# A linear-attention block and an MLP on one core: key weights folded once, first two pairs in 128-row products, a new order of the first stage

## The chip, the core and the metric

The kernel runs on one core of a Trainium2 chip. The metric is device time in microseconds (us), the median of the runs: 389.91 us before the change (3 runs, 389.55 to 390.11). Five engines work side by side, each through its own list of instructions in order: TensorE (PE; its weight loads are PEld), VectorE (DVE), ScalarE (ACT), GpSimd (POOL) and SyncE (SP), which only issues DMA transfers. ACT and POOL issue a few transfers too.

## The reference

x has 2048 rows (tokens) of 576 columns, 32 heads of 18 columns. All data are bfloat16.

```python
def _A_ref(x, wqkv, w_phi, wo):                       # H = 32, Dh = 18
    qkv = (x @ wqkv).reshape(B, S, 3, H, Dh).transpose(2, 0, 3, 1, 4)
    q, k, v = qkv[0], qkv[1], qkv[2]
    pq = einsum("bhsd,hdf->bhsf", q, w_phi)
    pk = einsum("bhsd,hdf->bhsf", k, w_phi)
    phi_q = concatenate([softmax(pq), softmax(-pq)], axis=-1)
    phi_k = concatenate([softmax(pk), softmax(-pk)], axis=-1)
    kv = einsum("bhsf,bhsd->bhfd", phi_k, v)          # over all tokens
    z  = einsum("bhsf->bhf", phi_k)
    num = einsum("bhqf,bhfd->bhqd", phi_q, kv)
    den = einsum("bhqf,bhf->bhq", phi_q, z)[..., None] + 1e-6
    return (num / den).transpose(0, 2, 1, 3).reshape(B, S, D) @ wo

def _B_ref(x, w1, b1, w2, b2):                        # 576 -> 4608 -> 576
    return gelu(layernorm(x) @ w1 + b1) @ w2 + b2

h  = x + _A_ref(layernorm(x), A_wqkv, A_w_phi, A_wo)
h2 = h + _B_ref(layernorm(h), B_w1, B_b1, B_w2, B_b2)
```

kv and z sum over all tokens, so no token's output can be finished before every token's keys and values are done.

## The kernel before

The 2048 tokens are 16 tiles of 128, handled as 8 pairs p = 0 to 7. The program has a first stage (mixer up to the state kv), a short tail that finishes the first pair, and the MLP blocks, between which the other pairs' mixer outputs are finished.

**Weights.** w_phi is folded into the key and query weights, so that x yields pk and pq in one product. For that the weights must lie transposed. The key weights wk are loaded and turned on PE (`flip_mm`, L377, evicted by `flip_ev`, L383), the query weights come through transposing DMAs (`turn_wq`, L159). `spread` (L231) makes the block-diagonal bd out of w_phi. `fold_k_mm` (L405) multiplies the turned key weights with bd for nine blocks of 128 rows of the folded weight wkp: blocks 0 to 3 are rows 0 to 511, blocks 4 to 7 the rows from 64 on, block 8 the last and the first 64. Both layouts are made by products. For the queries `fold_mm` (L419) makes five blocks, and `swap_q` (L434 to L438) copies the halves crosswise by DMA.

**A pair.** Layer norm: `stats` (DVE, L312 and L313), `power` (POOL), `centre` (POOL), `scale` (DVE L335 or ACT L290). Its result lies with the two token tiles interleaved in chunks of 64 columns, and is turned by a DMA (`turn_dma`, L342) or, for pair 0, by nine PE transposes (`turn_x_mm`, L359). Then the products, each 18 matmuls of 64 rows by 128 columns against 288 columns of weights (`project`, L450): a row half of the array works for each token tile, so two such matmuls run side by side. One such group is called a product here: `value_mm`, `key_mm`, `query_mm`, two per pair (the two halves of the heads). ACT evicts: `value_ev` (L460), `key_exp` and `query_exp` (two exponentials per product, L472). `key_sum` on DVE is a reduction (L501) and a reciprocal (L503), `key_weigh` divides (POOL or DVE, L507). `sums(p, a)` adds one token tile to the state in PSUM with 11 matmuls (L586).

**Tail.** After the last `sums`, `table` (DVE) copies the state; `combine_mm` (L673) and `divide` (DVE, L686) make the mixer output of pair 0, `turn_o_mm` turns it, `residual_mm` (L722) multiplies by wo, `residual_add`, `residual_stats`, `second`, `rescale` and `turn2_mm` prepare the MLP's input; `up` begins (L1161). Eight query products are left over to fill PE during this chain.

**Order.** Each engine's list follows an order written out by hand in the program (some 350 lines of calls), for all five engines. PSUM for the first stage is a pool `two` of three buffers of two banks each, handed out in turn; keys' exponentials have five buffers. `filler(n)` are n matmuls of no use that keep PE busy while it would wait. The space of the transposed and folded weights is that of the first half of w1, so `load_w1(0, ...)` can start only after the folds. The second half of w1 and w2 take the space of the values and keys, so they start after the last `sums` (`close_keys`).

Of the kernel before, what the change touches and what calls it, by code (L numbers as in the profile page):

```python
# [8 lines left out]
P = 128  # L9
# [6 lines left out]
D = 576  # L16
# [4 lines left out]
NC = 5  # L21
# [19 lines left out]
B1R = (NM + 15) // 16 * 16  # L41
GAP = P - COUNT[-1] * 2 * DH
# [3 lines left out]
def kernel(  # L46
# [43 lines left out]
    def leave_home(key):  # L90
# [22 lines left out]
        tc.tile_pool(name="two", bufs=3, space=bass.MemoryType.PSUM, reuse_waits="tile")  # L113
# [4 lines left out]
    exk_pool = kctx.enter_context(tc.tile_pool(name="exk_pool", bufs=5, side="left"))  # L118
# [15 lines left out]
    wTk = borrowed(NG, D).rearrange("p (g f) -> p g f", g=NG)  # L134
# [29 lines left out]
    def load_wk(part, eng):  # L164
        if part:
            eng.dma_start(wk[0:KH, 4, :], A_wqkv[512:D, D : 2 * D])
# [8 lines left out]
    def load_values(part, eng):  # L175
        if part < 2:
            eng.dma_start(
                wv[:, 4 * part : 4 * part + 4, :],
                A_wqkv[part * KH : part * KH + 512, 2 * D : 3 * D].rearrange(
# [4 lines left out]
        r0 = 512 if part == 2 else 0  # L184
        eng.dma_start(
            wv[(part - 2) * KH : (part - 1) * KH, 8, :], A_wqkv[r0 : r0 + KH, 2 * D : 3 * D]
        )
# [6 lines left out]
    def load_phi(eng):  # L194
        two_rows = wphi_rows[0 : 2 * 252, :].rearrange("(g p) f -> p g f", p=252)
        eng.dma_start(wph[:, 0:4:2, :], two_rows[0:P, :, :])
        eng.dma_start(wph[:, 1:4:2, :], two_rows[252 - P : 252, :, :])
        eng.dma_start(wph[0:72, 4, :], wphi_rows[504:576, :])
# [3 lines left out]
    load_phi(nc.scalar)  # L202
# [53 lines left out]

    def filler(n):
# [6 lines left out]
    def warm(n):  # L264
        pw = two.tile([P, 4, P], FP32, name="pw", tag="two")
        wide = ident[:, :].rearrange("p (o f) -> p o f", o=1).to_broadcast([P, 4, P])
        for _ in range(n):
            nc.tensor.matmul(pw[:, :, :], ident[:, :], wide, start=True, stop=True)

# [59 lines left out]
    def scale(p, i, eng):  # L329
        mv, rs = moments[p][:2]  # L330
        dst, src = lnb[p % 3][:, :, i, :], chunks(2 * p + i)
        if eng is act:
# [16 lines left out]
    def transposes(key, src, home=None):  # L349
# [3 lines left out]
        else:  # L353
            parts = [
                two.tile([P, 5 - e, P], BF16, name="pT", tag="two")[:, :, :] for e in range(2)
# [7 lines left out]
    def turned_back(key, dst, part, copy):  # L363
        copy(dst[:, 5 * part : 5 + 4 * part, :], flight[key][part])  # L364

# [5 lines left out]

    def flip_mm(g):
        f0, m = g * 126 - 2 * (g % 2), P if g < NG - 1 else 72
        pX = flight["w", g] = two.tile([P, DP], BF16, name="pX", tag="two")
        for c in range(NC):
            k = P if c < NC - 1 else KH
            nc.tensor.transpose(  # L377
                pX[:m, c * P : c * P + k], wk[:k, c, f0 : f0 + m], ident[:k, :k]
            )

    def flip_ev(g, copy):
        m = P if g < NG - 1 else 72
        copy(wTk[:m, g, :], flight["w", g][:m, 0:D])  # L383
# [3 lines left out]
    def folded_part(g, name, c, rows):  # L387
        n = GH[g] * DH
        flat = flight[name, c].rearrange("p b f -> p (b f)")
        return flat[rows, SPAN + g * 126 : SPAN + g * 126 + n]  # L390

    def folded_whole(name, c, m):
        return flight[name, c].rearrange("p b f -> p (b f)")[:m, SPAN : SPAN + D]

    def fold_k_mm(n):
        flight["k", n] = two.tile([P, 2, 512], FP32, name="pW", tag="two")[:, :, :]
        if n < 8:
            f0 = n // 4 * KH + n % 4 * P
            parts = [(slice(0, P), slice(f0, f0 + P))]
        else:  # L400
            parts = [(slice(0, KH), slice(512, D)), (slice(KH, P), slice(0, KH))]
        for g in range(NG):
            k = P if g < NG - 1 else 72
            for rows, fs in parts:
                nc.tensor.matmul(  # L405
                    folded_part(g, "k", n, rows), wTk[:k, g, fs],
                    bd[:k, g, 0 : GH[g], :].rearrange("p h f -> p (h f)"),
                    start=True, stop=True,
                )

    def fold_k_ev(n, copy):
# [909 lines left out]
```

## Time and profile before

| | |
|---|---|
| runs before, median | 389.91 us (389.55 to 390.11) |
| profiled execution, span | 391.7 us |
| first product of a value (PE) | 15.69 us |
| end of the last `sums` | 66.96 us |
| start of the MLP's first matmul | 86.00 us |
| PE busy | 383.0 us |

The profiled execution's own time is its span; it is 1.8 us above the median of the runs. A row of a view in order of time has the start, the length, the engine and the line, and in square brackets the idle time ahead and what ended it. In rows of groups, `x16 | 21.0, 1312 | 1.7` is 16 instructions, 21.0 us busy, 1312 ns mean, 1.7 us idle ahead. q8 is the DMA queue that brings instructions.

### The profile page before, as it was taken

What the parts mean: (1) busy time and instruction counts of PE and PEld (TensorE: products, weight loads), DVE (VectorE), ACT (ScalarE), POOL (GpSimd) and SP (SyncE); (2) the same over time, 40 slices, a digit from 0 to 9 for tenths busy, and PEclk for the clock granted to TensorE, in tenths of its full rate; (3) what the DMA queues carried; (4) which work ended last, traced back from release to release, by engine and by line L of the source; (5) the groups of instructions that cost most, each with busy time, mean ns of one, the idle gap of its engine ahead of it and who ended that gap; (6) DMA issues with size and microseconds to landing.
All of it is one profiled execution on the core that took longest, in us unless ns stands there. A gap on an engine that the chain in (4) does not pass through costs nothing.

```text
span 391.7 us, 10190 instructions
## 1 busy us (share of the span) xinstructions
PE 383.0 (98%) x4475; PEld 269.0 (69%) x4475; DVE 166.0 (42%) x364; ACT 163.2 (42%) x291; POOL 117.8 (30%) x161
## 2 busy tenths in 40 slices
PE   7999999799999999999999999999999999999997
PEld 3778779479978887844457887444677764447773
DVE  6998997385249388590019322000480000000100
ACT  2998995478500850046650000666300016661000
POOL 6399998116404654144003111000031110000120
PEclk9999999899999999999999999999999999999999
DMA  8977599999455578433003462000071000000000
GB/s 250 259 128 128 93 218 188 238 313 248 148 105 102 98 105 136 94 66 68 2 2 62 89 108 48 17 1 2 2 105 47 17 15 2 2 2 0 17 28 19
DMA packets 74096, 34.93 MB, mean 89 GB/s; under 512 B 61028, under 2 KB 71524, under 8 KB 74052
## 3 DMA queue, kind: packets, MB, share of 16 engines
q1 hardware_dynamic: 72944, 32.78, 40.3%
q0 software_dynamic: 336, 1.33, 1.2%
q8 instruction: 35, 0.57, 0.7%
q10 hardware_dynamic: 772, 0.17, 0.2%
q14 instruction: 9, 0.07, 0.1%
HBM read 16.47 MB, written 2.36 MB: 48 GB/s over the span
## 4 chain that ended last, share of the span: by engine, by line
PE 93%; ACT 2%; DMA 2%; issue 1%; DVE 1%; SPq 0%
PE po L1205 36%; PE ph L1161 36%; PE pk L450 8%; PE pv L450 5%; PE pa L722 4%; DMA w<-in_A_wqkv_dram 2%; PE acc_kv L586 1%; PE pn L673 1%; ACT home L472 1%; ACT shared L412 0%; DVE xh L731 0%; PE pW L419 0%; PE pW L405 0%; PE pT L359 0%; PE pX L377 0%
## 5 line engine op out<-in xcount | busy, mean ns | idle before, releaser
L1183 ACT ACTIVATE home<-ph,b1col 128x512 bf16<-128x512 f32 (+1 forms) x180 | 98.4, 598 | 169.1 <-PE ph L1161 165.9
L1205 PE MATMUL po<-w,home 128*128 128x288 bf16 (+2 forms) x1152 | 143.3, 286 | 0.0
L1161 PE MATMUL ph<-shared,w 64*128 64x512 bf16 (+2 forms) x1638 | 141.3, 331 | 0.6 <-ACT shared L364 0.6
L1205 PEld LDWEIGHTS <-home 128*128 128x128 bf16 x1152 | 109.4, 98 | 32.1 <-issue 1.8
L1161 PEld LDWEIGHTS <-w 64*128 64x128 bf16 x1638 | 80.3, 94 | 60.5 <-issue 0.7
L1209 DVE TENSOR_TENSOR ot<-po,hb 128x288 bf16<-128x288 f32 (+2 forms) x32 | 14.4, 453 | 106.4 <-PE po L1205 96.7
L450 PEld LDWEIGHTS <-home 64*128 64x128 bf16 x864 | 42.9, 95 | 13.6 <-issue 3.3
L1194 POOL TENSOR_TENSOR hb<-xh,b2bc 128x576 f32<-128x576 bf16 x16 | 20.4, 1273 | 104.6 <-DVE ot L1209 102.8
L536 POOL TENSOR_TENSOR padded<-home,rq 128x540 bf16<-128x540 bf16 x32 | 34.9, 1102 | 34.5 <-DVE rq L528 18.9
L731 DVE TENSOR_TENSOR xh<-pa,xh 128x288 bf16<-128x288 f32 x32 | 13.0, 447 | 72.4 <-PE pa L722 72.4
L274 POOL TENSOR_TENSOR rs<-va,mhalf 128x1 f32<-128x1 f32 x16 | 8.8, 549 | 110.9 <-DVE va L272 110.9
L507 POOL TENSOR_TENSOR phik<-phik,rk 128x576 bf16<-128x576 bf16 x28 | 33.4, 1218 | 1.4 <-DVE rk L503 1.2
L472 ACT ACTIVATE home<-pk 128x576 bf16<-128x576 f32 x32 | 18.6, 665 | 12.7 <-PE pk L450 10.4
L450 PE MATMUL pk<-wqp,home 64*128 64x288 bf16 x288 | 20.5, 293 | 2.8 <-issue 2.8
L501 DVE TENSOR_REDUCE sk<-phik 128x64 f32<-128x1152 bf16 x16 | 21.0, 1312 | 1.7 <-ACT phik L472 1.6
L527 DVE TENSOR_REDUCE sk<-home 128x64 f32<-128x1152 bf16 x16 | 21.0, 1310 | 0.0
L686 DVE RECIPROCAL rec<-pn 128x18 f32<-128x18 f32 (+1 forms) x32 | 8.0, 249 | 28.5 <-PE pn L673 28.5
L450 PE MATMUL pv<-wv,home 64*128 64x288 bf16 x288 | 19.6, 283 | 0.0
L472 ACT ACTIVATE phik<-pk 128x576 bf16<-128x576 f32 x32 | 18.7, 656 | 1.8 <-PE pk L450 1.1
L450 PE MATMUL pk<-shared,home 64*128 64x288 bf16 x288 | 19.3, 283 | 0.0
L722 PE MATMUL pa<-wo,shared 64*128 64x288 bf16 x288 | 18.6, 283 | 0.0
L722 PEld LDWEIGHTS <-shared 64*128 64x128 bf16 x288 | 13.9, 94 | 4.5 <-issue 0.5
(76 smaller groups left out, 208.3 us busy)
## 6 DMA issues: line engine op xcount, KB each, us to landing
w<-in_B_w_dram SPq DMA_DIRECT2D x21, 432.0 KB, 8.7
out_dram<-ot SPq DMA_DIRECT2D x15, 144.0 KB, 2.2
xh<-in_A_x_dram SPq DMA_DIRECT2D x3, 576.0 KB, 6.8
wo<-in_A_wo_dram SPq DMA_DIRECT2D x4, 324.0 KB, 8.0
w<-in_B_w_dram POOLq DMA_DIRECT2D x3, 432.0 KB, 13.0
wv<-in_A_wqkv_dram SPq DMA_DIRECT2D x2, 576.0 KB, 8.7
w<-in_A_wqkv_dram SPq DMA_DIRECT2D x1, 576.0 KB, 6.0
wqp<-wqp SPq DMA_DIRECT2D x2, 288.0 KB, 3.9
```

The lines of the kernel that those rows point to most:

```text
L450: nc.tensor.matmul(dst[:, a, 0:HALF], lhs[rows, c, :], w[rows, slot, i * HALF : (i + 1) * HALF], start=(n == 0), stop=(n == KC - 1),)
L472: nc.scalar.activation(rows[:, :, i * HH : (i + 1) * HH, s, :], flight[key, p, i][:, :, 0:HALF].rearrange("p a (h f) -> p a h f", f=DH), A ...
L501: nc.vector.tensor_reduce(sk[:, :, :], part_of(dst, i), AX.X, ALU.add)
L507: eng.tensor_tensor(part, part, flight["r" + key, p, i][:, a, :].rearrange("p (h o) -> p h o", o=1).to_broadcast([P, NH, DH]), ALU.mult,)
L527: nc.vector.tensor_reduce(sk[:, :, :], part_of(phiq[p], i), AX.X, ALU.add)
L536: eng.tensor_tensor(padded[:, a, g0 * P : (g0 + 5) * P].rearrange("p (g k) -> p g k", k=P)[:, :, 0:STEP].rearrange("p g (h f) -> p g h f", ...
L722: nc.tensor.matmul(pa[a], oT[p % 2][rows, c, :], wo[rows, c, cs], start=(c == 0), stop=(c == KC - 1),)
L1161: nc.tensor.matmul(ph[half][:, lo:hi], w1[p_ // 9][rows, c, p_ % 9 * P : (p_ % 9 + 1) * P], ln2T[rows, c, base + lo : base + hi], start=(c ...
L1183: nc.scalar.activation(hidden(m), ph[half][:, 0:width], AF.Gelu_apprx_tanh, bias=b1col[:, m : m + 1], scale=1.0,)
L1194: nc.gpsimd.tensor_tensor(hb[:, :], xh[:, t, :], b2bc[:, :], ALU.add)
L1205: nc.tensor.matmul(po[:, :], hidden(m)[:, i_ * P : (i_ + 1) * P], w2[m // 18][:, m % 18, cs], start=(j == 0), stop=(j == NM - 1),)
L1209: nc.vector.tensor_tensor(ot[:, cs], po[:, :], hb[:, cs], ALU.add)
```

## The change

Five things are changed.

1. **Key weights folded once.** `fold_k_mm` is gone. `fold_mm` makes five blocks for the keys as for the queries, and `swap_k` copies the halves crosswise by two DMAs. The last 64 rows of wk are loaded twice (`load_wk(1)`, `load_wk(2)`), so that the fifth flip has 128 rows.
2. **Pairs 0 and 1 in 128-row products** (NAT = 2). Their layer norm is kept in the natural order of columns, turned on PE (`turn_n_mm`: ten transposes a pair) and multiplied per token tile: four blocks of 128 rows times two halves of the columns, and a last block of 64 rows for both tiles side by side (`project_n`, `plain_tails`). Only the blocks that the folds write are needed for that, not the copies. `key_n_*`, `query_n_*` and `value_n_*` do the same work as before per token tile instead of per half of the heads.
3. **Named PSUM buffers.** `grab` takes the buffer that was given back first, `give` gives it back where its reader is written, in place of turns. The same for the keys' buffers and for the six banks of the MLP.
4. **wo in two loads** of 64 contiguous rows each in place of four of 32; `divide` places its output accordingly. w1's second half is loaded at places of the order instead of in one go.
5. **A new order** of the first stage and the tail. Fillers stand between the first turns and folds (48 in place of 32). `gelu_table` stands in the middle of the first stage.

```diff
+NAT = 2
-        tc.tile_pool(name="two", bufs=3, space=bass.MemoryType.PSUM, reuse_waits="tile")
+        tc.tile_pool(name="two", bufs=1, space=bass.MemoryType.PSUM, reuse_waits="tile")
...
+    def grab(kind, key, shape, dt):
+        n = held[kind, key] = free[kind].pop(0)
+        pool = {"two": two, "exk": exk_pool, "acc": later}[kind]
...
+        return pool.tile(shape, dt, name=f"{kind}{n}", tag=f"{kind}{n}")
+
+    def give(kind, key):
+        if (kind, key) in held:
+            free[kind].append(held.pop((kind, key)))
...
+    def turn_n_mm(p, a):
+        part = grab("two", ("x", p, a), [P, 4 + a, P], BF16)
+        flight["x", p, a] = part[:, :, :]
+        for n in range(4):
+            nc.tensor.transpose(
+                part[:, n, :], plain(p)[:, a, n * P : (n + 1) * P], ident[:, :]
+            )
+        if a:
+            for e in range(2):
+                nc.tensor.transpose(
+                    part[e * KH : (e + 1) * KH, 4, :], plain(p)[:, e, 512:D], ident[:, :]
+                )
...
     def fold_mm(name, c):
-        m = P if c < NC - 1 else 64
-        flight[name, c] = two.tile([P, 2, 512], FP32, name="pW", tag="two")[:, :, :]
+        flight[name, c] = grab("two", ("fold", name, c), [P, 2, 512], FP32)[:, :, :]
+        src = wTk if name == "k" else wTq
+        f0 = c * P if c < 4 or name == "k" else 448
         for g in range(NG):
             k = P if g < NG - 1 else 72
             nc.tensor.matmul(
-                folded_part(g, name, c, slice(0, m)),
-                wTq[:k, g, c * P : c * P + m],
+                folded_part(g, name, c), src[:k, g, f0 : f0 + P],
                 bd[:k, g, 0 : GH[g], :].rearrange("p h f -> p (h f)"),
                 start=True, stop=True,
             )
...
+    def swap_k(part):
+        if part:
+            nc.sync.dma_start(wkp[KH:P, 1:8:2, :], wkp[0:KH, 0:8:2, :])
+        else:
+            nc.sync.dma_start(wkp[0:KH, 1:8:2, :], wkp[KH:P, 0:8:2, :])
...
+    def project_n(key, p, a, w, slots, tail):
...
+        steps = [(slice(a * KH, (a + 1) * KH), 8, tail)] if tail is not None else [
+            (slice(0, P), 4 * a + n, slots[n]) for n in range(4)
+        ]
+        for k, (rows, block, slot) in enumerate(steps):
+            for i in range(2):
+                yield (
+                    dst[:, i, 0:HALF], turned(p)[rows, block, :],
+                    w[rows, slot, i * HALF : (i + 1) * HALF],
+                    done == 1 and k == 0, done == 2 and k == len(steps) - 1,
+                )
...
+    def plain_tails(key, p, w, tails):
+        both = [list(project_n(key, p, a, w, None, tails[a])) for a in range(2)]
+        multiply(step for pair in zip(*both) for step in pair)
...
-    def load_wo(part):
-        half, e = divmod(part, 2)
-        r0 = half * KH + e * 32
-        nc.sync.dma_start(
-            wo[r0 : r0 + 32, :, :], A_wo.rearrange("(h c e) f -> e h c f", c=KC, e=2)[e]
+    def load_wo(half, eng):
+        eng.dma_start(
+            wo[half * KH : (half + 1) * KH, :, :], A_wo.rearrange("(k c) f -> k c f", c=KC)
         )
...
-        for n in range(6):
-            load_w1(1, n, (nc.sync, nc.gpsimd)[n % 2])
...
+    fold_mm("k", 4)
+    fold_ev("k", 4, act)
+    key_n_mm(0, 0)
+    key_n_tail(0)
...
+    gelu_table()
+    key_mm(7, 1)
+    key_exp(7, 1)
```

ACT in the ramp, from its first table load to the first exponentials. Before (L290 is `scale`, L383 a flip, L364 turned x, L412 a key fold, L460 a value, L472 key exponentials):

```order
5 L223 ACT_TABLE_LOAD
6 L223 COPY spare<-mhalf 128x4
7 L290 ACTIVATE shared<-xh,nb,rs 128x9x64
8 L383 COPY w_0_108<-pX 128x576
9 L290 ACTIVATE shared<-xh,nb,rs 128x9x64
10 L383 COPY w_0_108<-pX 128x576
11 L364 COPY home_63<-pT 128x512
12 L412 CAST shared<-pW 128x576 x7
13 L290 ACTIVATE shared<-xh,nb,rs 128x9x64
14 L412 CAST shared<-pW 128x576
15 L460 CAST vals<-pv 128x2x16x18
```

and of the change (L309 is `scale`, L426 a flip, L413 turned x, L453 a fold, L570 exponentials of one token tile):

```order
6 L309 ACTIVATE shared<-xh,nb,rs 128x576
7 L426 COPY w_0_108<-two_216 128x640
8 L426 COPY w_0_108<-two_232 128x640
9 L426 COPY w_0_108<-two_243 72x640
10 L413 COPY home_63<-two_250 128x640
11 L453 CAST shared<-two_273 128x576
12 L453 CAST shared<-two_297 128x576
13 L453 CAST shared<-two_314 128x576
14 L453 CAST shared<-two_321 128x576
15 L309 ACTIVATE shared<-xh,nb,rs 128x576
16 L570 ACTIVATE exk_349<-two_328 128x32x18 x2
17 L413 COPY home_63<-two_353 128x640
```

Eight key folds on ACT became four; the first eviction after them is a key's exponential in place of a value.

SP where the first half of w1 (`w_0_108`), wo and b2 are loaded and the queries of pair 0 are turned (shared<-padded). Before (w_1 and w_0_1868 are the second half of w1 and w2, after the last `sums`):

```order
26 L624 DMA wo<-in_A_wo_dram 32x9x576 x2
27 L572 DMA_TRANSPOSE shared<-padded 128x11x128 x2
28 L624 DMA wo<-in_A_wo_dram 32x9x576
29 L613 DMA w_0_108<-in_B_w_dram 64x3x1152 x2
30 L638 DMA b2bc<-in_B_b_dram 128x576
31 L613 DMA w_1_1867<-in_B_w_dram 64x3x1152 x3
32 L619 DMA w_0_1868<-in_B_w_dram 128x3x576 x6
```

and of the change (home<-shared are turned pairs):

```order
28 L779 DMA b2bc<-in_B_b_dram 128x576
29 L363 DMA_TRANSPOSE home_66<-shared 128x9x128
30 L754 DMA w_0_108<-in_B_w_dram 64x3x1152
31 L363 DMA_TRANSPOSE home_65<-shared 128x9x128
32 L765 DMA wo<-in_A_wo_dram 64x5184
33 L754 DMA w_0_108<-in_B_w_dram 64x3x1152
34 L708 DMA_TRANSPOSE shared<-padded 128x11x128 x2
35 L754 DMA w_0_108<-in_B_w_dram 64x3x1152
36 L754 DMA w_1_1549<-in_B_w_dram 64x3x1152 x2
37 L762 DMA w_0_1550<-in_B_w_dram 128x3x576 x3
```

b2, wo and all but one of SP's parts of the first half of w1 stand ahead of pair 0's turned queries now; the other half of wo and one part of w1 are issued by ACT.

ACT in the middle of the first stage, of the change alone:

```order
53 L530 CAST vals<-two_1028 128x2x16x18
54 L926 ACT_TABLE_LOAD
55 L926 ACTIVATE spare<-mhalf 128x4
56 L543 ACT_TABLE_LOAD
57 L543 ACTIVATE exk_1068<-two_1049 128x2x16x18 x2
```

The gelu table is loaded and the exponentials' table right after it; before, the gelu table was loaded once, after the last exponential.

More of the change, by code (lines that the diff above doesn't have):

```diff
@@ L354, in transposes @@
             parts = [
-                two.tile([P, 5 - e, P], BF16, name="pT", tag="two")[:, :, :] for e in range(2)
+                grab("two", (key, e), [P, 5 - e, P], BF16)[:, :, :] for e in range(2)
             ]
@@ L364, in turned_back @@
         copy(dst[:, 5 * part : 5 + 4 * part, :], flight[key][part])
+        give("two", (key, part))
     def turn_x_mm(p):
@@ L580, in sums @@
         left.remove(t)
+        last = t + 1 - 2 * a not in left
         for w in range(KW):
@@ L591, in sums @@
             )
+        if last:
+            give("exk", p)
     def table(b):
```

873 lines of the change are left out of this document (486 added, 387 removed).

## The prediction

> **What bounds the kernel now.** I read the page first, then the busy time by stage, then the chain of waits in order of time.
>
> ```profile
> span 391.7 us, 10190 instructions
> PE 383.0 (98%) x4475; PEld 269.0 (69%) x4475; DVE 166.0 (42%) x364; ACT 163.2 (42%) x291; POOL 117.8 (30%) x161
> q8 instruction: 35, 0.57, 0.7%
> ```
>
> ```profile
> 8.36:15.69 7.33, 7.01 (x101) 5.74 (x103) 6.61 (x19) 6.55 (x12) 2.71 (x8) 1.00 1.16 305
> 15.69:66.96 51.27, 51.27 (x923) 42.39 (x925) 46.63 (x69) 45.03 (x79) 45.48 (x55) 1.00 0.81 154
> 66.96:70.60 3.64, 3.64 (x67) 2.60 (x66) 2.61 (x10) 1.65 (x3) 2.07 (x3) 1.00 1.06 210
> 70.60:73.37 2.77, 0.00 (x1) 0.01 (x2) 1.02 (x3) 0.74 (x2) 0.00 (x0) 1.00 1.07 216
> 73.37:77.40 4.03, 4.03 (x39) 2.68 (x41) 0.82 (x2) 1.19 (x2) 0.00 (x0) 0.58 1.04 251
> 77.40:86.00 8.60, 8.03 (x128) 6.28 (x125) 6.49 (x19) 6.16 (x12) 1.10 (x2) 1.00 1.06 301
> 86.00:391.70 305.70, 303.01 (x3196) 206.53 (x3195) 96.49 (x229) 99.79 (x182) 61.74 (x72) 1.00 0.29 59
> ```
>
> Columns: stretch, length, then busy time of PE, PEld, DVE, ACT, POOL, the granted clock, DMA share, GB/s. From 86.00, where the MLP begins, TensorE is busy without a gap and the change leaves that work alone: 305.7 us stay. From 15.69 (first product) to 66.96 (last state sum, called M below) PE is full too, but DVE, ACT and POOL are all near 90%, so M can be set by any of them. Between M and 86.00 lie 19.04 us, and there the chain shows something else:
>
> ```profile
> 22.41 2.20 PE pv L450 x36
> ...
> 63.71 3.25 PE acc_kv L586 x110
> 66.96 1.21 PE pk L450 x18
> ...
> 70.60 2.77 issue
> 73.37 0.86 PE pk L450 x10
> 74.23 1.07 PE pT L359 x9
> 75.30 2.23 PE pk L450 x18
> ...
> 283.17 35.39 PE po L1205 x288
> ```
>
> PE stops for 2.77 us in the middle of a product, waiting for no engine; then 10 products, 9 transposes and 18 products take 4.16 us at half clock. At full clock they take 0.61 + 0.68 + 1.10 = 2.39 (61 ns a product by 22.41; nine transposes by 10.70 below). So this hole costs 2.77 + 1.8 = **4.5 us**, and 19.04 - 4.5 = 14.5 us is the tail without it. Its cause I read from the DMA rows of 64.5 to 70 and of 70 to 72:
>
> ```profile
> q1 hardware_dynamic: 833, 1.22, 103.7%
> ...
> q1 hardware_dynamic: 277, 0.44, 103.9%
> q8 instruction: 1, 0.02, 4.3%
> ```
> ```profile
> 62.61 0.84 SPq L624 DMA_DIRECT2D wo<-in_A_wo_dram  x1
> 63.51 1.30 SPq L613 DMA_DIRECT2D w<-in_B_w_dram  x2
> 64.85 0.61 SPq L638 DMA_DIRECT2D b2bc<-in_B_b_dram  x1
> ```
>
> The 35 packets of q8 carry PE's 8950 instructions, 256 each. No block arrives for 5.5 us while 324 + 2 x 432 + 144 KB of weights are queued; one arrives just as PE stands still. PE crosses a block about every 256 instructions (near its 2237th it ran dry, so also near 1981 and 2493). If PE asks for a block on entering the one before, the block that lacked at 70.60 was asked for near 1981, the 99th of the 220 instructions of the 110 sums (about 65.2 us), and was usable at 73.37: **8.2 us** under full DMA.
>
> **The change, part by part.**
>
> Work on PE hardly changes. A 128-row product of 288 columns costs 123 ns (283.17), two 64-row ones 2 x 61 = 122: 96 + 24 products replace 216 at no gain. Removed: 25 key fold products. Added: 16 fillers, 11 transposes, each some 60 ns (estimate from nine transposes in 0.68 us): +0.1 us in all.
>
> The ramp moves. Rows:
>
> ```profile
> 8.36 2.41 PE L377 MATMUL pX<-ident,w 128*128 128x128 bf16 x25 [0.92 <-DMA w<-in_A_wqkv_dram]
> 10.70 0.68 PE L359 MATMUL pT<-ident,shared 128*128 128x128 bf16 x9
> 11.97 4.02 ACT L412 CAST shared<-pW 128x576 bf16<-128x576 f32 x7
> ...
> 81.02 4.46 ACT L472 ACTIVATE home<-pk 128x576 bf16<-128x576 f32 x8 [2.25 <-DVE st L739]
> L290 ACT ACTIVATE shared<-xh,nb,rs 128x576 bf16<-128x576 bf16 x9 | 8.0, 886 | 3.3 <-POOL nb L284 3.3
> ```
>
> The flips wait for the key weights. Now 288 KB of x lie behind these and 72 KB more ahead: 216 KB less at some 230 to 305 GB/s, 0.7 to 0.9 us earlier. Fillers and four transposes of x then hold PE to about 7.9. ACT evicts two flips, the last flip, x and four folds (8 x about 0.6 = 4.8 us), so the first key product can start near 12.5 instead of 15.69. On PE: 12.5 + 51.27 + 0.9 (fillers within) + 0.5 (turns of pair 1) = 65.2; but the 17.4 us of PE work on pairs 0 and 1 hang, through three PSUM buffers, on ACT, which owes there 16 exponentials (0.56 each), 11 casts and copies (0.57) and 5 scalings (about 0.8): 19.2 us. The last of it trails PE; I put the wait at 1.2: M = 66.4 by PE. By DVE:
>
> ```profile
> 9.30:65.00 55.70, 55.38 (x949) 45.56 (x949) 52.86 (x87) 51.32 (x89) 46.33 (x61) 1.00 0.85 166
> 4.81 0.77 DVE L312 BATCH_NORM_STATS2 st<-xh 128x6 f32<-128x288 bf16 x2
> 5.74 0.77 DVE L312 BATCH_NORM_STATS2 st<-xh 128x6 f32<-128x288 bf16 x2
> 54.28 1.29 DVE L501 TENSOR_REDUCE sk<-phik 128x64 f32<-128x1152 bf16 x1
> 56.09 1.29 DVE L501 TENSOR_REDUCE sk<-phik 128x64 f32<-128x1152 bf16 x1
> 59.75 5.25 DVE L507 TENSOR_TENSOR phik<-phik,rk 128x576 bf16<-128x576 bf16 x4
> L335 DVE TENSOR_SCALAR shared<-xh,mv,rs 128x576 bf16<-128x576 bf16 x7 | 3.7, 522 | 0.0
> L412 DVE CAST shared<-pW 128x576 bf16<-128x576 f32 x1 | 0.7, 702 | 0.0
> ```
>
> I put the end of DVE's two flip copies at 9.3, some 1.4 us after the flips begin. It then still owes 14 token tiles of statistics (0.93 from one to the next: 13.0), 6 scales (3.1), 18 sums with reciprocals (1.81: 32.6), four weighings (5.25), one fold and one value eviction (1.4): 55.4 us, against 52.9 done from there to 65.0 before. It ends at 64.7 with no wait, and after two more sums of 11 products (22 of 110 in 3.25 us: 0.7) M = 65.4. Before, DVE waited 2.8 us in that stretch; with as much M = 68.2. PE's 66.4 lies between, and waits that fall on both at different times add up: I take 0.6 more, **M = 67.0, as before** (65.4 to 68.2). So the earlier first product buys nothing: DVE has more left to do at that point.
>
> ACT: one fold fewer here, but the gelu table now loads in the middle, the exponential table again, and gelu again at the first gelu.
>
> ```profile
> L223 ACT ACT_TABLE_LOAD x1 | 1.3, 1283 | 3.0 <-issue 3.0
> ```
>
> Two more loads, 2.6 us: ACT had 6.2 us idle between 15.69 and 66.96, and the last one is covered by three pairs of PSUM banks in the MLP. Nothing, at most 2.6. The key copies on SP (2 x 288 KB) have until pair 4's keys, some 15 us: nothing. Named buffers: nothing by themselves; the MLP's 303.01 of 305.70 leave no gain, and a bank that comes free late would cost under 1.
>
> The tail is the same work and chain (table, two combines, divide, turn, residual, norm, turn): 14.5. What changes is DMA. Before M, b2, three more w1 parts and both wo halves are queued early; only two w1 parts (864 KB) remain near the last sums. Block 1981 now falls in the combine, asked for early in the 110 sums: the rest of these 3.25 us, waits for DVE and one product later PE needs it, about 6 us. With 864 KB queued instead of 1332 the 8.2 us shrink to 8.2 x 0.65 = 5.3: in time. Block 2237 falls some 9 us after M, in the fifth query product of the tail, asked for at 1981, near M + 1.5: 7.6 us, now under the full flood of w1's second half; 8.2 leaves 0.6 short, and nothing is short if service is a little faster. I take 0.5. Bounds: 0 and a whole hole again, 4.5.
>
> **Sum**: 67.0 + 14.5 + 0.5 = 82.0 for the MLP's start against 86.0: -4.0, span 387.7. The profiled execution is 391.7, the median of the runs 389.91, 1.8 below; the same step off the median gives **385.9 us**.
>
> Here the Trainium skill bears, "Runtime: NRT & Kernel Launch", section on instruction fetch mechanics: a block of 16 KiB holds 256 instructions, and crossing into the next is mostly hidden. The size agrees with q8's 0.57 MB in 35 packets; "hidden" does not agree with 2.77 us here. If the rule held, the gap would have another cause and would return, as in the first rival.
>
> **Rivals.**
>
> First, the hole only moves: block 2237 comes as late as the one before, since w1's nine loads still go out together after M. For it: DMA share stays above 1.0 all the way from 66.96 to 86.00. Against: the sums, which ate 220 instructions in 3.3 us, no longer lie inside the wait. Price: 4.5 instead of 0.5: 389.9, no change.
>
> Second, slower: both blocks are late. If service takes 8.2 us at both, 1981 is 2.2 short and 2237 0.6 short, and each gap halves the clock (1.8 each): 6.4 instead of 0.5, 391.8. It decides from the point where w1's last two parts and the turns of q are still queued as the 110 sums start. Against: wo is gone by then. "TensorE: Matmul & The Clock Gate" in the Trainium skill (what's actually happening) has the clock halve after an idle window of about 3.4 us; the trace halves it after 2.77, so its row decides.
>
> Third, the ramp is later: query folds now stand on PE's queue ahead of pair 1's keys and need the transposed loads of the query weights by about 15.7 us; at 3 us late, PE, ACT and DVE all shift by 2 to 3, and DVE waits as before: M = 70 to 72, 389 to 391. For it: DMA is above 1.0 from 8.36 to 15.69. Against: these loads are issued some 12 us earlier than before.
>
> **Chances.** Forecast (384.3 to 388.0) 0.55, first rival 0.17, second 0.13, third 0.15. This measurement can tell about 0.2%, 0.8 us, from no change. Faster: 0.55 + 0.02 + 0 + 0.05 = 0.62. Same: 0.11 + 0.03 = 0.14. Slower: 0.04 + 0.13 + 0.07 = 0.24. The range 384.0 to 391.0 leaves out the second rival and less than a tenth below; the forecast's own, from M's bounds and a gap of 0 to 1, is 384.3 to 388.0.
>
> **What would show it.** After: first key product near 12.5, DVE full from 9.3 on and its last weighing near 66, M near 67.0, MLP's start near 82.0, no "issue" gap above 1 us in the tail and full clock there, the MLP 305.7. Wrong: a gap without a releaser after M (first or second rival), or M beyond 69 with DVE waiting (third).

## The result

The changed kernel takes **393.66 us** (median of 4 runs, 393.26 to 393.81) against 389.88 for the kernel before (4 runs). The ratio is 1.0095, 95% interval 1.0076 to 1.0113: 3.8 us slower, where 385.9 was forecast and 384.0 to 391.0 given as the range.

The changed kernel's profiled execution has a span of 391.8 and a time of 393.55. The span of the profile before was 391.7 although its kernel is 3.8 us faster, so that profile can't be what the kernel usually does. Two later executions of the kernel before lasted 805.22 and 1024.13 us; they are left out of the spans and ratios below. A second profile of the unchanged kernel before (first experiment below) has a span of 388.9. The comparison is made with that one. By stage, the second profile of the kernel before (stretch, length, busy time of PE, PEld, DVE, ACT, POOL, granted clock, DMA share, GB/s):

```profile
15.44:66.90 51.46, 51.46 (x923) 41.52 (x925) 46.63 (x69) 45.10 (x79) 45.55 (x55) 1.00 0.84 157
66.90:82.19 15.29, 14.03 (x229) 10.63 (x230) 11.17 (x33) 9.75 (x18) 3.17 (x5) 1.00 1.05 234
82.19:101.03 18.84, 18.14 (x343) 16.18 (x343) 7.26 (x9) 15.67 (x37) 8.70 (x11) 1.00 1.11 307
101.03:164.71 63.68, 63.68 (x833) 51.67 (x834) 41.89 (x103) 15.89 (x38) 23.88 (x30) 1.00 0.58 103
164.71:388.90 224.19, 221.45 (x2024) 137.21 (x2024) 47.21 (x118) 68.38 (x108) 29.30 (x32) 1.00 0.16 31
```

The same stages of the changed kernel, same columns:

```profile
12.69:69.45 56.76, 54.33 (x853) 42.41 (x854) 48.65 (x82) 49.45 (x83) 45.53 (x54) 1.00 0.87 179
69.45:83.68 14.23, 13.88 (x229) 10.75 (x230) 10.31 (x31) 8.83 (x17) 3.19 (x5) 1.00 0.96 216
83.68:103.36 19.68, 18.51 (x343) 17.59 (x343) 7.93 (x10) 16.68 (x38) 8.54 (x11) 1.00 1.12 259
103.36:167.76 64.40, 64.06 (x832) 52.04 (x834) 42.35 (x103) 15.94 (x38) 23.98 (x30) 1.00 0.62 110
167.76:391.80 224.04, 221.45 (x2025) 137.20 (x2024) 47.61 (x118) 68.28 (x108) 29.25 (x32) 1.00 0.15 31
```

| stage | before | after | difference |
|---|---|---|---|
| end of the last state sum (M) | 66.90 | 69.45 | +2.55 |
| tail, to the first MLP product | 15.29 | 14.23 | -1.06 |
| first MLP block, products with w1 | 18.84 | 19.68 | +0.84 |
| from there to the start of the third block | 63.68 | 64.40 | +0.72 |
| the rest | 224.19 | 224.04 | -0.15 |
| span | 388.9 | 391.8 | +2.9 |

The loss is in three places, M and the two MLP stages, and each has its rows. M first: the chain of waits of the changed kernel, start and length of each piece.

```profile
47.35 0.53 ACT vals L530
...
47.90 1.28 ACT L926
...
49.41 1.28 ACT L543
...
51.25 0.65 ACT exk L543
...
51.95 3.48 PE two L480 x54
```

L926 is the early load of the gelu table, the second 1.28 the exponential table that has to come back for the next `key_exp`. TensorE has nothing to do from 49.78 to 51.95, 2.17 us. A sentence of the Trainium skill ("ScalarE: Activation LUTs", "What ACT_TABLE_LOAD costs") gives 1283 ns for a load, as measured here, and some 1380 ns of drain for each switch on top; the rows show next to none of that second part, only 0.20 for the dummy gelu between the two loads.

The first MLP block, in the chain of waits of the changed kernel:

```profile
84.17 2.10 PE acc L1326 x48
86.28 0.28 issue
86.55 7.25 PE acc L1326 x128
93.81 0.86 issue
94.67 8.69 PE acc L1326 x156
```

Two stops ("issue": the profile shows nothing that TensorE waited for, no releaser), 1.14 us. In the second profile of the kernel before, TensorE stops in this stage once too, for 0.70 us up to 87.11:

```profile
86.35 0.47 ACT home L1183
86.82 0.28 issue
87.11 13.93 PE ph L1161 x251
```

The view puts this down to ACT, but ACT had ended 0.28 us before TensorE went on. So of the 0.84 us the stops explain some 0.44; TensorE's busy time is 0.37 longer too (18.51 against 18.14), and why, no run shows. The second block of the changed kernel, same view:

```profile
137.12 0.28 DVE rec L826
...
139.51 0.48 DVE ob L827
...
140.03 2.03 PE acc L1326 x33
```

TensorE waits 0.34 us for a division to leave a PSUM bank. The stage is 0.72 longer; experiment 6 gives all but 0.1 of that back.

### The profile page after: what moved, and what is told of

Its sections match the earlier page's. It is cut to its first block, busy times and chain, and to the rows that moved or that the text cites. A ratio compares the mean times of both kernels' runs of the same rounds, so it can differ in the third digit from the quotient of the medians.

```text
span 391.8 us, 10004 instructions
## 1 busy us (share of the span) xinstructions
PE 383.4 (98%) x4381; PEld 267.2 (68%) x4381; DVE 164.7 (42%) x362; ACT 165.4 (42%) x292; POOL 117.8 (30%) x162
## 4 chain that ended last, share of the span: by engine, by line
PE 94%; ACT 3%; DVE 1%; issue 1%; POOL 0%; POOLq 0%
PE acc L1371 36%; PE acc L1326 36%; PE two L480 8%; PE acc L863 4%; PE two L506 3%; PE two L286 1%; PE acc_kv L723 1%; DVE ob L827 1%; PE pn L813 1%; PE acc_kv L277 1%; PE two L863 1%; PE two L442 1%; PE acc L813 0%; DVE rec L826 0%; ACT exk L543 0%
## 5 line engine op out<-in xcount | busy, mean ns | idle before, releaser
L1348 ACT ACTIVATE home<-acc,b1col 128x512 bf16<-128x512 f32 (+1 forms) x180 | 98.1, 599 | 170.5 <-PE acc L1326 167.9
L1326 PE MATMUL acc<-shared,w 64*128 64x512 bf16 (+2 forms) x1638 | 142.3, 331 | 1.6 <-issue 1.1
L1371 PE MATMUL acc<-w,home 128*128 128x288 bf16 (+2 forms) x1152 | 143.3, 286 | 0.0
L1375 DVE TENSOR_TENSOR ot<-acc,hb 128x288 bf16<-128x288 f32 (+2 forms) x32 | 14.5, 453 | 106.4 <-PE acc L1371 100.7
L611 POOL TENSOR_TENSOR exk<-exk,rk 128x576 bf16<-128x576 bf16 x20 | 24.5, 1250 | 4.1 <-DVE rk L607 4.1
L605 DVE TENSOR_REDUCE sk<-exk 128x64 f32<-128x1152 bf16 x12 | 15.9, 1325 | 4.7 <-ACT exk L543 4.7
L480 PE MATMUL two<-wv,home 64*128 64x288 bf16 x216 | 14.4, 283 | 2.2 <-ACT exk L543 2.2
L863 PE MATMUL acc<-wo,shared 64*128 64x288 bf16 x252 | 16.4, 283 | 0.0
L297 DVE TENSOR_SCALAR shared<-xh,mv,rs 128x576 bf16<-128x576 bf16 x32 | 16.1, 566 | 0.0
L480 PE MATMUL two<-wqp,home 64*128 64x288 bf16 x216 | 14.6, 283 | 0.0
```

The costliest lines, as they stand in the source:

```text
L297: nc.vector.tensor_scalar(dst, src, mv[:, i, 0:1], rs[:, i : i + 1], ALU.subtract, ALU.mult)
L480: nc.tensor.matmul(dst[:, a, 0:HALF], lhs[rows, c, :], w[rows, slot, i * HALF : (i + 1) * HALF], start=(n == 0), stop=(n == KC - 1),)
L605: nc.vector.tensor_reduce(sk[:, :, :], part_of(dst, i), AX.X, ALU.add)
L611: eng.tensor_tensor(part, part, flight["r" + key, p, i][:, a, :].rearrange("p (h o) -> p h o", o=1).to_broadcast([P, NH, DH]), ALU.mult,)
L863: nc.tensor.matmul(pa[a], oT[p % 2][rows, c, :], wo[rows, c, cs], start=(c == 0), stop=(c == KC - 1),)
L1326: nc.tensor.matmul(ph[half][:, lo:hi], w1[p_ // 9][rows, c, p_ % 9 * P : (p_ % 9 + 1) * P], ln2T[rows, c, base + lo : base + hi], start=(c ...
```

## The experiments

The ratios are all to the kernel before, run beside the kernel of the experiment on the same chip, with 95% intervals.

**1. The kernel before once more.** No edit.

> The kernel before, without an edit, for its spans. After the change every execution lasts 1.75 us longer than its span (393.55 against 391.8, 393.26 against 391.5), while the profiled execution before had a span of 391.7 and its runs a median of 389.9. Theory A: the time stands 1.75 above the span in this kernel too, so its usual span is near 388.1, and the stop of 2.77 us with 1.8 us of half clock after it is not in the usual execution, or only in part. Theory B: the stop is in every execution, spans are 391.5 to 392, and time and span stand differently to each other in the two kernels.

Ratio 0.9986 (0.9969 to 1.0003): two copies of one kernel differ by that much. Its ten spans are 387.0 to 388.9. Over all experiments there are 98 executions of the kernel before whose span is known: 387.0 to 390.4, median 388.4, and in every one the time stands 1.66 to 1.79 above the span. Theory A holds. The execution of the profile before (391.7) lies above all 98. In two of the 98, both with a span of 390.3, the mean granted clock is 0.995 as it is in that profile, and in no other below 0.999: so the clock seems to halve for a while in a few executions of the kernel before too; where in those two, no trace shows. The stop of 2.77 us with the half clock behind it isn't in the second profile; the same place of the program there:

```profile
66.90 1.21 PE pk L450 x18
...
71.65 0.68 PE pT L359 x9
72.32 1.21 PE pk L450 x18
```

**2. The gelu table at the end again.**

```
     value_ev(2, 0, act)
-    gelu_table()
     key_mm(7, 1)
...
     query_exp(5, 1)
+    gelu_table()
     load_w2(0, 2)
```

> The changed kernel with the load of the gelu table moved from the middle of the key stage back to the end of the tail. Theory A: the two table loads (1.28 us each at 47.90 and 49.41) stand in the chain of waits where TensorE stops for 2.45 us at 49.5 for an eviction by ACT, and make the last state sum late; without them it ends near 67.0 instead of 69.45 and the time falls by 2.0 to 2.6 us, to about 391.3. Rival B: ACT is late there in any case (three PSUM buffers wait on it through the whole stage), the wait only shifts, and the time changes by less than 0.8 us.

391.38, ratio 1.0036 (1.0017 to 1.0055), 0.6 points less than the changed kernel: 2.3 us. The last sum ends at 67.02 and TensorE is full from 31.94 on:

```profile
12.60:31.94 19.34, 19.07 (x218) 13.70 (x218) 18.83 (x44) 18.68 (x32) 14.86 (x24) 1.00 0.88 217
31.94:67.02 35.08, 35.08 (x639) 28.32 (x640) 30.19 (x40) 27.90 (x49) 30.85 (x31) 1.00 0.95 173
```

Theory A, to its number. The rows also tell what sets M without the loads: TensorE (54.15 of 54.42 us), with VectorE at 49.01 and ACT at 46.58.

**3. The w1 load ahead of w2.**

```
+    load_w1(1, 2, syn)
     load_w2(0, 2)
     load_w2(0, 1)
     load_w2(0, 3)
-    load_w1(1, 2, syn)
     load_w2(0, 4)
```

> The changed kernel with the third of six loads of w1's second half issued ahead of the first three loads of w2 instead of behind them. Theory A: the stop of 1.13 us at 93.54, in the ninth pair of the first MLP block on its seventh product, is the wait for exactly this load; it goes, and the time falls by 0.9 to 1.2 us, to about 392.6. Rival B: the stop is a late block of instructions (one landed at 92.05); it stays within 0.3 us and the time within 0.3 us.

392.67, ratio 1.0062 (1.0040 to 1.0083): 1.0 to 1.3 us less, with intervals that just overlap, and the stop at the product that first reads this load (the seventh of pair 9, counted from 0) is gone, as theory A says. But its reason doesn't hold. In the changed kernel's trace this load is issued at 72.66 and has landed by 91.01 (18.4 us, the longest of its line), 2.8 us before the stop at 93.81 begins. The stop comes exactly 128 products behind the one at 86.28, and 128 products with their weight loads are 256 instructions, one block; and the kernel of experiment 2, with the w1 load behind w2, has no stop there. That the load's first use falls on the same product is chance. The stop is rival B's late block: the packet of q8 that lands from 92.05 on ends at 93.16, and TensorE goes on at 94.67. That the stop didn't stay, as rival B expected, suggests that the order of the loads has a say in when the block is fetched. TensorE passes the border before at 86.55 in the changed kernel and at 88.06 here, and the packet starts 5.5 and 2.8 us after it; but this execution runs 1.5 us later, and which of the two counts, no run shows.

In three of its seven executions the clock over the whole span is 0.996. In the profiled one it halves behind the table loads, which it didn't in the profiled execution of the changed kernel. This kernel:

```profile
52.24:57.40 5.16, 5.16 (x57) 3.98 (x56) 4.27 (x5) 3.19 (x6) 3.65 (x4) 0.67 0.77 150
```

The changed kernel, the same 54 products:

```profile
51.95:55.43 3.48, 3.48 (x56) 3.03 (x56) 3.41 (x4) 3.18 (x6) 2.39 (x3) 1.00 1.02 207
```

**4. The division as before.** The old order of elements in `divide`, and the four loads of wo that belong to it.

```
-        o = ob[...].rearrange("p c (h e) -> p c e h", e=2)
+        o = ob[...].rearrange("p c (e h) -> p c e h", e=2)
-                pv[:, :, 0:DH].rearrange("p h (e c) -> p c e h", e=2),
+                pv[:, :, 0:DH].rearrange("p h (c e) -> p c e h", e=2),
...
-        eng.dma_start(
-            wo[half * KH : (half + 1) * KH, :, :], A_wo.rearrange("(k c) f -> k c f", c=KC)
-        )
+        for e in range(2):
+            r0 = half * KH + e * 32
+            eng.dma_start(
+                wo[r0 : r0 + 32, :, :], A_wo.rearrange("(h c e) f -> e h c f", c=KC, e=2)[e]
+            )
```

> The changed kernel with the order of elements in the division, and the four loads of wo that go with it, as before. Theory A: each of the 32 divisions gets 0.06 to 0.07 us shorter (0.56 to 0.50, 0.49 to 0.42); four stand in the chain of the first tail, and TensorE waits 0.6 us for one near 139, so the time falls by 0.3 to 0.8 us. Rival B: in the first tail the two more loads of wo on the same queue take the gain back, and beside the MLP the divisions are hidden: less than 0.3 us either way.

394.81, ratio 1.0112 (1.0072 to 1.0153). Two of its four executions have a clock of 0.995 over the whole span, as executions with the half clock do; the other two, 393.37 and 393.98, lie with the changed kernel's. The divisions do get shorter (0.50, 0.42 instead of 0.57, 0.48), and nothing is gained: rival B.

**5. Both edits of 2 and 3 together.**

> The changed kernel with two edits together: the gelu table loaded at the end of the tail again, and the third load of w1's second half ahead of w2. Theory A: the two losses lie one after the other on TensorE's path and add up: 2.2 and 1.0 us less than 393.66, so 390.4, the last state sum near 67.0, no wait in the ninth pair of the first MLP block, and the ratio to the kernel before 1.000 +- 0.002. Rival B: the wait for the w1 load was there only because all work was 2.5 us late; then the two overlap and the time stays near 391.4, a ratio of 1.0036.

391.21, ratio 1.0032 (1.0017 to 1.0046): rival B. With the tables out of the way the w1 edit brings nothing that can be measured. The reason given with rival B (that load is late because all is late) isn't shown: this kernel's profiled execution has its stops at two other borders of blocks, so a stop can go at one border and come at another.

**6. The banks of a combine given back one pair later,** on top of 5.

```
         give("two", ("pn", t))
-        for b in range(2):
-            give("acc", ("pn", t, b))
+        owed.extend(("pn", t, b) for b in range(2))
...
                 give("acc", ("h", p0, p_, half))
+            settle()
...
                 give("acc", ("o", t, c0))
+                settle()
```

`settle` gives back what is owed, behind each pair of the products with w1 and each bank of those with w2.

> The kernel of the last experiment, in which the two PSUM banks of a combine are put back on the list of free banks one pair later, so that the third pair behind a combine takes other banks than those the division still reads. Theory A: the named banks make TensorE wait 0.6 us for a division in the second MLP block (139.4 to 140.0), and the stretch from the first down product to the third block gets shorter by 0.6 to 0.7 us, from 64.4 to 63.7 as before the change; the time falls by as much. Rival B: the wait moves to the pair whose banks are then the oldest, less than 0.2 us.

390.57, ratio 1.0011 (0.9996 to 1.0026): 0.6 to 0.8 us less. The place in the second block where TensorE waited for the division, in its chain of waits:

```profile
135.37 0.31 PE acc L819 x11
135.68 6.10 PE acc L1331 x108
```

The products run through; from the first product with w2 to the third block it is 63.76 (101.64 to 165.40). The intervals of 5 and 6 overlap, but this stretch is 64.4 in the profiles of kernels 2, 3 and 5 and 63.8 in all from 6 on. Theory A.

**7. Without 16 fillers,** on top of 6: the four `filler(4)` behind `key_n_tail(0)` are taken out.

> The kernel of the last experiment without the 16 filler products behind the first key products (they write a bank that nothing reads then). Theory A: TensorE sets the end of the key stage, because it never stops from 18 us to the last sum; 8 of the 16 fillers stand on that path (0.33 and 0.23 us in the chain), the others in a wait for ACT, so the last sum comes 0.5 to 0.7 us earlier and the time falls by that. Rival B: VectorE or ACT sets the end, as the sum of the prediction had it from DVE's side; TensorE waits for them instead and the time changes by less than 0.2 us.

389.56, ratio 0.9989 (0.9975 to 1.0003): 0.9 to 1.0 us less, while the last sum ends at 66.86 instead of 67.11, 0.25 earlier. So theory A's gain is there and its reason gives a quarter of it. The profiled execution with the fillers (kernel 6) has this in its tail:

```profile
75.76 1.34 PE two L486 x21
77.11 1.28 issue
78.39 3.36 PE two L486 x51
```

Without them (kernel 7):

```profile
75.52 4.41 PE two L486 x72
```

**8. One fold later,** on top of 7: the first fold of the query weights, and its eviction, behind pair 1's key tails.

```
     key_n_mm(0, 1)
-    fold_mm("q", 4)
...
-    fold_ev("q", 4, act)
...
     key_n_exp(1, 1)
+    fold_mm("q", 4)
+    fold_ev("q", 4, act)
     fold_mm("q", 3)
```

> The kernel of the last experiment with the first fold of the query weights and its eviction moved behind the tails of pair 1's key products. Theory A: the wait of 1.9 us at 16.05 is ACT's queue: two exponentials (1.20) and the eviction of this fold (0.64) stand ahead of the buffer that TensorE needs; without the eviction the wait is 0.6 us shorter, the last sum and the time come 0.4 to 0.6 us earlier. Rival B: ACT has the same work in the end, and the eviction that moved is waited for one buffer later: less than 0.2 us.

390.51, ratio 1.0010 (0.9993 to 1.0026): 0.9 us more than kernel 7. Neither theory: the last sum comes 0.93 us later (67.79). In kernel 7 TensorE did the five products of that fold while it waited for ACT; now it waits all the same, and does them afterwards:

```profile
17.84 0.59 ACT home L419
18.42 1.11 ACT exk L576 x2
...
19.57 0.43 PE two L448 x5
```

**9. The 16 fillers again, in a wait,** on top of 7: `filler(16)` ahead of `key_n_tail(1)`.

> The kernel without the 16 fillers, with 16 fillers put back in one place where TensorE waits for ACT in any case (ahead of the tails of pair 1's key products, a wait of 1.9 us). TensorE then has as many instructions as with the fillers in their old places, and every later block of 256 instructions begins at the same piece of work as there. Theory A: what the fillers cost was not their own time (the last sum moved by 0.25 us, the time by 1.0), but that they moved the borders of the instruction blocks, so that one fell into the tail at 77 us, where the block came 0.9 to 1.3 us late; the time goes back up by 0.7 to 1.0 us, to a ratio of 1.001, and the spans spread over 1.7 us again instead of 1.0. Rival B: the fillers cost their own time on the path; hidden in a wait they cost nothing, and the ratio stays at 0.999.

390.62, ratio 1.0017 (0.9997 to 1.0038), spans 388.1 to 390.2 (kernel 7: 387.3 to 388.3). In its chain of waits:

```profile
68.67 0.42 PE two L819 x11
69.09 0.09 PE pn L819 x3
69.18 0.69 issue
69.87 0.39 PE pn L819 x8
70.26 2.31 PE two L486 x36
72.57 0.61 PE pT L386 x9
73.18 1.21 PE two L486 x18
74.39 2.20 PE two L868 x36
76.59 1.34 PE two L486 x21
77.94 0.38 issue
```

Two stops without a releaser are back, at the very places where kernels 2 and 5 have them (behind the third product of the combine's second bank, and behind the twenty-first of the queries after the residual, where kernel 6 stops too). Between the two lie 8 + 36 + 9 + 18 + 36 + 21 = 128 products, 256 instructions. That is theory A, with a reserve: the last sum also came 0.6 us later, so the fillers weren't hidden, and of the 1.7 us by which the profiled span is longer the two stops are 1.07. Of the 1.06 us between the medians, up to 0.6 can thus be the fillers' own time; that the stops come back, and where, is what speaks for theory A.

**10. One scaling on GpSimd,** on top of 7.

```
-    centre(1, 1)
-    scale(1, 1, act)
+    scale(1, 1, pool)
```

> The kernel without the 16 fillers, with one scaling of pair 1's tokens (0.77 us on ACT, from 13.51 to 14.28 in the chain of waits) moved to GpSimd, where its inputs are ready from 12.5. Theory A: from 9.4 to 18.5 the start of the key stage hangs on ACT's queue; with 0.77 us less there, the first turn of pair 1 and the waits at 16.0 and 17.2 come 0.4 to 0.8 us earlier, TensorE is full behind them, and the last sum and the time fall by 0.4 to 0.7 us, to a ratio of 0.9975. Rival B: the eviction that TensorE waits for at 17.9 hangs on VectorE or GpSimd too, or GpSimd's weighings come later and are waited for: less than 0.2 us.

390.09, ratio 1.0001 (0.9985 to 1.0018): no gain. GpSimd takes 2.30 us for what ACT does in 0.77, and TensorE waits for it:

```profile
12.85 2.30 POOL shared L362
...
15.20 0.40 PE two L409 x4
```

That isn't all: in this profiled execution, the slowest of ten, TensorE waits another 0.89 us for transposed tokens (up to 38.07), which kernel 7's profile doesn't show, and the last sum comes at 68.8. I had taken its price from GpSimd's weighings (1.16 for the same 576 elements) without saying so; that row doesn't hold for this form.

**11. The changed kernel once more.** No edit.

> The changed kernel, without an edit, beside the kernel before on the same chip. Theory A: its loss is steady, because it lies in the order of the work (the table loads, the w1 load, the bank, the fillers) and not in chance: ratio 1.008 to 1.011, and in some executions the stop of 2.4 us at 49.5 is followed by a stretch at half clock, as it is seen in the kernel with the early w1 load, which costs 1.7 us more. Rival B: the loss was that of one chip and its block fetches: ratio under 1.005.

394.09, ratio 1.0096 (1.0063 to 1.0129): theory A. The loss is steady. In its profiled execution, the slowest of five, the clock halves behind the table loads (5.15 us for the 54 products); there TensorE also waits 0.74 us for parts of w2 (up to 109.03 and 110.18).

**12. That scaling on VectorE,** on top of 7: `scale(1, 1, vec)` and no `centre(1, 1)`.

> The kernel without the 16 fillers, with the scaling of pair 1's tokens that stands in ACT's chain (0.77 us) moved to VectorE, where the same scaling takes 0.38 us, instead of to GpSimd, where it took 2.30. Theory A: it was GpSimd's duration alone that spoiled the step; on VectorE the operand is ready at 13.3, before TensorE comes to it at 14.0, ACT has 0.77 us less ahead of the waits at 16.0 and 17.2, and the last sum comes 0.4 to 0.7 us earlier, near 66.2: ratio 0.9975 to 0.998. Rival B: VectorE is full from 8 to 16 us (7.65 of 8.00) and sets the end of the key stage, as the prediction had it as one bound; the last sum stays at 66.8 or comes later, ratio 0.999 or above.

389.46, ratio 0.9976 (0.9960 to 0.9993): the one kernel that is faster than the one before by more than its interval. Two copies of the kernel before came out at 0.9986 (experiment 1), so this is little more than chance can give. The ratio is theory A's, the mechanism isn't shown: the interval overlaps that of kernel 7, and the profiled execution, the slowest of twelve, has its last sum at 68.2, because there TensorE waits 1.11 us for transposed tokens, as in experiment 10:

```profile
32.07 5.36 DMA home<-shared
```

The kernels that were built one on the other:

| kernel | ratio | 95% interval |
|---|---|---|
| changed kernel | 1.0095 | 1.0076 to 1.0113 |
| 2: gelu table at the end | 1.0036 | 1.0017 to 1.0055 |
| 5: and w1 ahead of w2 | 1.0032 | 1.0017 to 1.0046 |
| 6: and banks one pair later | 1.0011 | 0.9996 to 1.0026 |
| 7: and 16 fillers fewer | 0.9989 | 0.9975 to 1.0003 |
| 12: and one scaling on VectorE | 0.9976 | 0.9960 to 0.9993 |

## Why the prediction was wrong

The span was forecast at 387.7 and is 391.8; the time was put 1.8 below the span and is 1.75 above it. That is 4.1 + 3.6 of the 7.7 us between 385.9 and the profiled 393.55.

**"The profiled execution is 391.7, the median of the runs 389.91, 1.8 below; the same step off the median": this step failed first.** A time of which the span is a part can't be below it; that the profile's span was above the median said that its execution was a rare one. In all 98 executions the time is 1.7 above the span, so the profiled execution's own time isn't its span, as the table of the kernel before has it, but near 393.4. A usual span before was thus near 388.2, and 3.5 us of the 4.5 us "hole" were never in the time that was to be improved. With that, the same sum gives 387.7 + 1.7 = 389.4, no change within 0.2%, close to the first rival's 389.9.

**The hole's cause was right, its weight wrong.** TensorE's stops without a releaser in the tail and the first MLP block lie, kernel by kernel, on a grid of 128 products, the borders between blocks of 256 instructions. The stop before (2.77, 163 products ahead of the MLP) and a short one in the second profile (0.03 us in its chain, 36 ahead) are 127 apart, which would be one record short of a block. The packets of q8 in the traces show the cause itself: at each of these stops TensorE goes on 1.3 to 1.8 us after a packet has ended. Some of them:

| profile | packet of q8 | TensorE goes on | stop |
|---|---|---|---|
| kernel before | 70.25 to 71.62 | 73.37 | 2.77 |
| kernel before, once more | 84.64 to 85.75 | 87.11 | 0.70 |
| changed kernel | 83.87 to 84.93 | 86.55 | 0.28 |
| changed kernel | 92.05 to 93.16 | 94.67 | 0.86 |
| kernel 6 | 75.69 to 76.93 | 78.39 | 1.28 |
| kernel 9 | 67.22 to 68.47 | 69.87 | 0.69 |

Where a packet had ended more than 1.8 us before TensorE came to the border, none of the 14 profiles has a stop there between 43 and 103 us. So the blocks do come late, by 0 to 1.3 us in these profiles and 2.8 in one. The Trainium skill ("Runtime: NRT & Kernel Launch", "Instruction fetch mechanics") has blocks of 256 instructions and a crossing that is mostly hidden: the first agrees with the grid of 128 products and their weight loads, the second with most crossings, not with those in the table.

The premise that a block is asked for on entering the one before agrees with the traces too: at the border that TensorE passes at 43 to 52 us, the packet of the next block starts within 0.7 us of it in all 14 profiles. In the tail it starts up to 6.8 us after the border (kernel 6). The estimate of 8.2 us from one border to the next usable block holds for the stop that it was worked out from (8.3 in the trace), but it is no constant: at the stops this time lies between 4.9 and 9.5 us. The blocks that the prediction placed at 1981 and 2237 are at instructions 1977 and 2234 of the traces. Kernels 2, 5 and 9 stop at both (0.43 and 0.10, 0.25 and 0.93, 0.69 and 0.38 us) without a half clock after them, which is the second rival in kind with 0.5 to 1.2 us where it had 6.4; the changed kernel stops at neither.

**"Two more loads ... ACT had 6.2 us idle ... Nothing, at most 2.6": the term that was mis-sized.** It cost 2.43 at M (69.45, and 67.02 without the early load in experiment 2), close to its own upper bound. ACT's idle time of a whole stage was set against a delay in one place, where all three PSUM buffers stood in ACT's queue and TensorE had nothing else. Nor did the early load save one later, as the prediction saw: the last exponentials come just ahead of the first gelu, so the table is loaded there again. The chain of waits of kernel 3, which has the early load too, with the last exponentials, the load and the first gelus:

```profile
86.09 0.99 ACT home L543 x2
...
87.20 1.28 ACT L1348
...
88.50 0.85 ACT home L1348 x2
```

**M = 67.0 was right without the loads** (67.02 in experiment 2), and so were the first key product (12.5 forecast, 12.69), and the flips (7.9; 8.21). But it was the TensorE bound, not a mean of two: 54.4 us from the first key product where the sum had 53.9. In experiment 2 no wait of TensorE for VectorE of 0.1 us or more shows in this stretch, so the 0.6 us put on top for waits that add up has no row of its own, and that 67.0 was met so closely is partly luck. VectorE owed 55.4 us from 9.3 on by the sum, at prices from one start to the next; in experiment 2 it was busy for 52.2 of 57.7 (9.30 to 67.02), idle for 5.5, and not the limit. "So the earlier first product buys nothing: DVE has more left to do" names the wrong engine: what the earlier start gave went into fillers, turns and the waits for ACT at 16 to 18.

**The tail** (15.0 with the 0.5 for a block) took 14.23; the tail of the second profile before is 15.29, where 14.5 was worked out. Of the 1.06 us, 0.86 are two waits of TensorE that got shorter: for a division (0.50, now 0.31) and for ACT ahead of the MLP (0.71, now 0.04). **"The MLP 305.7"** became 308.1. "A late bank would cost under 1" was right as a bound: it cost 0.6 to 0.8, and was taken at nothing. The stops in the first MLP block (1.14) are the first rival in kind, blocks late at other borders: near 2493, which the prediction lists but does not price, and one block later. The kernel before has 0.70 near the second of these. The third rival's sign, M beyond 69, came true by another cause.

## What to carry to other kernels

Before a profile is costed, set its span against the spans or times of other executions: if it is longer than the median time, the profile shows a rare event, and no change can earn what that event cost. Idle time of an engine over a stage doesn't cover a delay put into its queue at one point; ask which buffers wait behind that point and whether the engine that needs them has other work. Instructions that cost nothing by their duration still move the borders of the instruction blocks behind them; where the queues are full, compare kernels with the same number of instructions ahead of that stretch.

## What the runs showed of the hardware

- The same stop of TensorE, 2.17 us behind the table loads, halves the granted clock in some executions (0.67 over the 5.16 us behind it, 1.7 us more) and not in others: in 6 of the 20 executions of the changed kernel and kernels 3 and 4 the clock over the whole span was 0.995 or 0.996; in the 82 executions of kernels 2, 5 to 10 and 12, which load no table there, it never was below 0.999. A stop behind table loads isn't the only way: the kernel before, which loads none there either, had 0.995 in 2 of 98 executions. The Trainium skill ("TensorE: Matmul & The Clock Gate", "What's actually happening") has a window of some 3.4 us that runs freely; that the same stop sometimes counts and sometimes doesn't agrees with a free window, that 2.17 us can be enough does not agree with a whole idle window of 3.4.
- Late blocks of instructions stop TensorE at fixed instructions 256 apart, by up to 1.3 us and in one profile 2.8, and not alike from one execution to the next (0.86 and 0.16 us at one border in two profiles of the changed kernel). TensorE goes on 1.3 to 1.8 us after the end of the packet of q8 (14 stops of 0.1 us or more). With 16 fillers fewer the stops were gone from the tail, and with 16 elsewhere they were back; but the changed kernel and kernels 3 and 4, which have the fillers and come to the tail some 2 to 4 us later, pass these borders without a stop. What holds a packet back at one border (6.8 us behind the border before in kernel 6) and less at another (4.4 in kernel 7) is open.
- A scaling with two per-partition operands over 576 bf16 elements takes 0.40 us on VectorE, 0.88 on ACT (0.77 from one to the next) and 2.29 on GpSimd.
